# Four small memsets of a constant move from GpSimd to VectorE at the start of a fused attention and gated FFN kernel

## The chip, the cores and the metric

The kernel runs on one core of one Trainium2 chip. The metric is the device time of one launch in microseconds (us). The time before is the median of three runs, 517.77 us (517.19 to 517.79).

The engines are named as in the profile: PE is TensorE's matrix multiplication and PEld its weight load, DVE is VectorE, ACT is ScalarE, POOL is GpSimd, SP is SyncE. [...]

## The reference

Attention with keys and values projected to 64 positions (Linformer), followed by a gated FFN:

```python
# q, k, v: (8, 8, 1024, 64); E, F: (64, 1024); all float32
k_proj = einsum('ks,bhsd->bhkd', E, k)
v_proj = einsum('ks,bhsd->bhkd', F, v)
scores = (1 / sqrt(64)) * matmul(q, k_proj.transpose(0, 1, 3, 2))
attn = softmax(scores)
x = matmul(attn, v_proj).transpose(0, 2, 1, 3).reshape(8192, 512)
gate = 1 / (1 + exp(-(x @ w_gate)))          # w_gate, w_val: (512, 1536)
out = (gate * (x @ w_val)) @ w_out           # w_out: (1536, 512)
```

The output is (8192, 512) in float32.

## The kernel before, in words

**Tiling.** A batch has 1024 positions, which are handled as two blocks of 512 tokens. Per batch the kernel projects k and v with E and F, forms the scores, takes the exponential on ACT, multiplies by the projected v, normalizes, and runs the FFN over the two blocks: 12 column tiles of 128 for the gate and the value, then the output projection. From the second block on, a growing part of the FFN's products is computed in a Strassen-like form with fewer multiplications, with the sums on DVE and copies on ACT. Matmuls are in bf16, with sums in PSUM in float32. The bulk of the kernel (from the third block on) is ordered by a planner with costs and due times (`arranged`). The start, which the change touches, is not: it runs in the order in which the code records it.

**How order and waits come about.** Each operation is recorded by `Plan.add` with keys that it reads (`r`) and writes (`w`). Every engine executes its own operations in the order of recording. `add` looks up, for each key, the writers and readers recorded so far, and makes the new operation wait for them: a read waits for the earlier writer, a write waits for earlier writers and earlier readers. Waits within DVE are left out for a write after a read, waits across engines never are. A DMA counts on a semaphore of its own; other operations that somebody waits for count on their engine's semaphore.

**The start.** The calls come in this order:

```python
start_loads()
blocks_ready(0)
constants()
project_consts()
busy(4)
```

- `start_loads` (L472) issues the loads of E and F on SP (L476). On POOL it sets `quad` by four memsets of 32 partitions each, to 0, 32, 64 and 96 (L482), and then issues 22 loads through `load` (L403): k, q, k, q, v, v for the halves of the heads of batch 0, then pieces of the gate and value weights with two more of q among them.
- `blocks_ready(0)` (L914) sets `kpd`, which is used from batch 2 on, to zero on POOL. It names `quad` among the keys that it reads, though it doesn't touch that tile.
- `constants` (L504) works on DVE alone: `count` (0 to 127 in each row, by doubling, L505 and L509), four patterns (L515 to L533), their transpose `rows` (L545), `row_f` (the partition's number, a row number plus `quad`, L553), the identity matrices `identf` and `ident` (L559), `half` (L567), the selectors `dsel8` (L576), `bsel8f` and `bsel8` (L592).
- `project_consts` (L604) transposes E and F on PE with `identf`; ACT copies the result to `EFT`.
- `busy(n)` (L628) puts n matmuls of `ident` with itself into PE's order; nothing uses their result. Four follow the transposes, and ten more stand between the steps of the first half unit.
- The first half unit then projects k of batch 0 for half of the heads, transposes q and the projected k, forms scores and so on, up to `xT` (L868), the FFN's input. The FFN's first products (L385 with wG and wV) follow.

All matmuls are recorded at L385, all ACT operations of the helper at L389.

Of the kernel before, what the change touches and what calls it, by code (L numbers as in the profile page):

```python
# [121 lines left out]
class Plan:  # L122
# [31 lines left out]
    def add(self, eng, fn, r=(), w=(), x=(), dma=None, t=None, tie=(), pad=0.0):  # L154
        if self.tasks is not None:
            self.note(eng, (eng, fn, tuple(r), tuple(w), tuple(x), dma), t, tie, pad)
            return None
        op = Op()
        op.eng, op.fn, op.dma, op.need = eng, fn, dma, False
        op.sem, op.val = None, 0  # L160
        deps = {}

        def dep(o, raw):
            if o is op:
                return
            if o.eng == eng and o.dma is None:
                if eng == "PE" or (eng != "POOL" and not raw):
                    return
            deps[id(o)] = o

        for k in r:
            for o in self.writers.get(k, ()):
                dep(o, True)
        for k in tuple(w) + tuple(x):
            for o in self.writers.get(k, ()):
                dep(o, False)
            for o in self.readers.get(k, ()):
                dep(o, False)
        for k in r:
            self.readers.setdefault(k, []).append(op)  # L180
        for k in tuple(w) + tuple(x):
            self.writers[k] = [op]
            self.readers[k] = []
        op.deps = list(deps.values())
        for o in op.deps:
            o.need = True
        if dma is not None:
            self.dma_count[dma] = self.dma_count.get(dma, 0) + 16
            op.sem, op.val = dma, self.dma_count[dma]
        self.ops.append(op)  # L190
        return op
# [46 lines left out]
def bass_linformer_attn__then__ffn_glu_sigmoid_kernel(  # L238
# [18 lines left out]
    with contextlib.ExitStack() as es:  # L257

        def sbuf(name, shape, dtype):
            return es.enter_context(nc.sbuf_tensor(name, shape, dtype))  # L260
# [38 lines left out]
        quad = sbuf("quad", [P, 1], FP32)  # L299
# [91 lines left out]
        def dve(fn, r, w, b=None, t=None):  # L391
            x = [] if b is None else [("bank", b)]
            return add("DVE", fn, r=r, w=w, x=x, t=t)

        def pool(fn, r=(), w=()):
            return add("POOL", fn, r=r, w=w)
# [33 lines left out]
        def load_kv_heads(n, src, R):  # L430
            hh = slice(4 * R, 4 * R + 4)
            load(
                KV[n][:, hh, :],
                src[0].rearrange("h (p t) d -> p h (t d)", t=NT)[:, hh, :],
                [("KV", n, R)],
                f"KV{n}{R}",
            )
# [34 lines left out]
        def start_loads():  # L472
            for src, rows, n in ((E, slice(0, 64), "E"), (F, slice(64, 128), "F")):
                add(
                    "SP",
                    lambda e, src=src, rows=rows: e.dma_start(EF[rows, :], src[:, :]),  # L476
                    w=[("EF", n)],
                    dma="in" + n,
                )
            for i in range(4):  # L480
                pool(
                    lambda e, i=i: e.memset(quad[32 * i : 32 * i + 32, :], 32.0 * i),  # L482
                    w=[("quad", i)],
                )
            for R in range(2):
                load_kv_heads(0, k, R)
                load_q_half(0, 0, R)
            for R in range(2):
                load_kv_heads(1, v, R)
            load_w(0, 0)  # L490
            load_w(0, 1)
            load_w(1)
            load_w(2)
            for R in range(2):
                load_q_half(0, 1, R)
            load_w(3)
            load_w(4)
            load_w(5)

        def heads8():  # L500
            x = count[:, 0:8].rearrange("p (h b) -> p h b", h=2)
            return x.unsqueeze(2).to_broadcast([P, 2, 4, 4])

        def constants():  # L504
            dve(lambda e: e.memset(count[:, 0:1], 0.0), [], ["count"])  # L505
            for i in range(7):
                n = 1 << i
                dve(
                    lambda e, n=n: e.tensor_scalar(  # L509
                        count[:, n : 2 * n], count[:, 0:n], float(n), None, op0=ALU.add  # L510
                    ),
                    ["count"],
                    ["count"],
                )
            dve(lambda e: e.tensor_copy(pats[:, 0, :], count[:, 0:32]), ["count"], ["pats"])  # L515
            dve(
                lambda e: e.tensor_copy(
                    pats[:, 1, :].rearrange("p (h a b) -> p h a b", h=2, b=4),
                    heads8(),
                ),  # L520
                ["count"],
                ["pats"],
            )
            dve(
                lambda e: e.tensor_copy(
                    pats[:, 2, :].rearrange("p (a b) -> p a b", b=4),
                    count[:, 0:4].unsqueeze(1).to_broadcast([P, 8, 4]),
                ),
                ["count"],
                ["pats"],  # L530
            )
            dve(
                lambda e: e.tensor_scalar(  # L533
                    pats[:, 3, :].rearrange("p (a b) -> p a b", b=16),
                    count[:, 0:16].unsqueeze(1).to_broadcast([P, 2, 16]),
                    8.0,
                    -1.0,
                    op0=ALU.is_ge,
                    op1=ALU.mult,
                ),  # L540
                ["count"],
                ["pats"],
            )
            dve(
                lambda e: e.transpose(  # L545
                    rows[:, :, :].rearrange("p a b -> p (a b)"),
                    pats[:, :, :].rearrange("p a b -> p (a b)"),
                ),
                ["pats"],
                ["rows"],  # L550
            )
            dve(
                lambda e: e.tensor_tensor(row_f[:, :], rows[:, 0, 0:1], quad[:, :], ALU.add),  # L553
                ["rows"] + [("quad", i) for i in range(4)],
                ["row_f"],
            )
            for t, n in ((identf, "identf"), (ident, "ident")):
                dve(
                    lambda e, t=t: e.tensor_scalar(  # L559
                        t[:, :], count[:, :], row_f[:, 0:1], None, op0=ALU.is_equal  # L560
                    ),
                    ["count", "row_f"],
                    [n],
                )
            for n, op in ((0, ALU.is_ge), (1, ALU.is_lt)):
                dve(
                    lambda e, n=n, op=op: e.tensor_scalar(  # L567
                        half[:, n : n + 1], row_f[:, :], 64.0, None, op0=op
                    ),
                    ["row_f"],  # L570
                    [("half", n)],
                )
            for n in range(2):
                for i in range(4):
                    dve(
                        lambda e, n=n, i=i: e.tensor_scalar(  # L576
                            dsel8[:, n, i, :].rearrange("p (h a b) -> p h a b", h=2, b=4),
                            heads8(),
                            half[:, n : n + 1],
                            2.0 * i,  # L580
                            op0=ALU.subtract,
                            op1=ALU.is_equal,
                        ),
                        ["count", ("half", n)],
                        [("dsel8", n)],
                    )
            for t, k, m, i, v in (
                (bsel8f, "bsel8f", 8, 1, 0.25),
                (bsel8, "bsel8", 8, 1, 0.5),
            ):  # L590
                dve(
                    lambda e, t=t, m=m, i=i, v=v: e.tensor_scalar(  # L592
                        t[:, :, :, :].rearrange("p c h d -> p (c h) d"),
                        count[:, 0:m].unsqueeze(2).to_broadcast([P, m, 64]),
                        rows[:, i, 0:1],
                        v,
                        op0=ALU.is_equal,
                        op1=ALU.mult,
                    ),
                    ["count", "rows"],  # L600
                    [k],
                )
# [1525 lines left out]
```

The softmax here doesn't subtract the row's maximum and nothing guards it: scores larger than these inputs give would overflow.

## Time and profile before

| what | us |
|---|---|
| median of three runs | 517.77 |
| the profiled execution | 517.65 |
| its span | 515.90 |
| PE busy | 505.0 |
| DVE busy | 410.9 |
| ACT busy | 345.0 |
| POOL busy | 41.0 |
| PE's first matmul starts | 5.86 |
| DVE's first instruction starts | 0.82 |
| POOL's quad memsets | 0.75 to 1.31 |
| POOL's memset of kpd | 18.32 to 19.28 |
| v's first half lands | 17.26 |

The span runs from the first to the last thing that the profile shows; the execution's own time is 1.75 us longer. Starts are counted from the span's start. A line of the timeline gives the start, the busy time, the engine, the source line, the operation, the tile written and the one read, the number of instructions, and in brackets how long the engine stood idle and what released it. PE's records overlap, because matmuls are pipelined. A queue name with q at its end (POOLq, SPq) stands for an engine's sequencer. The granted clock of PE is given as 1.0 in all stages.

### The profile page before, as it was taken

The numbers are of one execution on the slowest core, as the hardware profiler recorded it, in microseconds if no ns is written. First come the engines' busy times: TensorE is split into PE (matmuls) and PEld (weight loads), VectorE is DVE, ScalarE is ACT, GpSimd is POOL, SyncE is SP. The second block draws the span as 40 slices with busy tenths as digits, with TensorE's granted clock in tenths as the row PEclk, the third lists the DMA queues.
The fourth block names the chain that finished last, engine by engine and source line by source line (L and its number), as shares of the span: only waits on it lengthen the run. The fifth ranks groups of instructions, "written<-read, shape, count | busy, mean of one in ns | idle before, by whom it ended". The sixth has DMA issues, their size and how long they took to land.

```text
span 515.9 us, 11369 instructions
## 1 busy us (share of the span) xinstructions
PE 505.0 (98%) x4598; PEld 410.0 (79%) x4598; DVE 410.9 (80%) x809; ACT 345.0 (67%) x645; POOL 41.0 (8%) x60
## 2 busy tenths in 40 slices
PE   5999999999999999999999999999999999999996
PEld 3545645888888888888888888888888888888885
DVE  4548779899789796988879888797969898777774
ACT  2555683867778677677767776777676766676652
POOL 9420301200200020000100020000000000000000
PEclk9999999999999999999999999999999999999999
DMA  9999999899798788454946389374104330201013
GB/s 161 199 198 204 150 195 221 115 178 233 93 224 155 152 150 138 102 125 123 174 85 154 60 152 203 56 164 100 46 7 97 42 104 1 83 1 76 6 43 124
DMA packets 105205, 63.13 MB, mean 122 GB/s; under 512 B 63040, under 2 KB 97344, under 8 KB 105152
## 3 DMA queue, kind: packets, MB, share of 16 engines
q0 software_dynamic: 34000, 29.89, 37.5%
q1 hardware_dynamic: 71152, 32.52, 28.8%
q8 instruction: 36, 0.59, 0.4%
q14 instruction: 17, 0.14, 0.1%
HBM read 60.29 MB, written 16.78 MB: 149 GB/s over the span
## 4 chain that ended last, share of the span: by engine, by line
PE 94%; DMA 2%; DVE 1%; POOL 1%; issue 0%; ACT 0%; DVEq 0%; POOLq 0%
PE pA L385 51%; PE pF L385 43%; DMA KVs<-in_v_dram 2%; DVE hT L1832 0%; POOL KVs L403 0%; DVE vsnap L1710 0%; POOL Qb L403 0%; DVE xT L868 0%; DVE ost L1437 0%; ACT sig L389 0%; DVE sig L1786 0%; ACT vsnap L389 0%; DVE ost L1522 0%; POOL quad L482 0%; DVE hS L1382 0%
## 5 line engine op out<-in xcount | busy, mean ns | idle before, releaser
L389 ACT ACTIVATE sig<-pA 128x512 f32<-128x512 f32 x126 | 75.1, 596 | 43.4 <-PE pA L385 42.8
L1699 ACT ACTIVATE pF<-pA 128x512 f32<-128x512 f32 x99 | 58.5, 591 | 30.9 <-PE pA L385 26.3
L1710 DVE TENSOR_TENSOR vsnap<-pF,vsnap 128x512 f32<-128x512 f32 x90 | 61.8, 686 | 18.1 <-ACT vsnap L389 9.2
L1786 DVE TENSOR_TENSOR sig<-pF,sig 128x512 f32<-128x512 f32 x84 | 57.5, 685 | 7.2 <-PE pA L385 3.7
L385 PE MATMUL pF<-wO,hT 128*128 128x256 bf16 (+1 forms) x402 | 59.3, 285 | 0.0
L389 ACT ACTIVATE vsnap<-pA 128x512 f32<-128x512 f32 x84 | 50.2, 597 | 11.9 <-PE pA L385 11.8
L1832 DVE SCALAR_TENSOR_TENSOR hT<-sig,vsnap 128x512 bf16<-128x512 f32 x84 | 56.6, 683 | 0.9
L389 ACT ACTIVATE sig<-sig 128x512 f32<-128x512 f32 x84 | 52.8, 629 | 2.9 <-DVE sig L1786 2.6
L385 PE MATMUL pF<-xS,wV 128*128 128x256 bf16 x360 | 54.0, 273 | 0.1
L385 PE MATMUL pA<-xT,gT 128*128 128x256 bf16 x336 | 50.4, 273 | 0.0
L385 PE MATMUL pF<-xS,wG 128*128 128x256 bf16 x336 | 50.4, 273 | 0.0
L385 PE MATMUL pA<-xT,vT 128*128 128x256 bf16 x336 | 50.4, 273 | 0.0
L385 PE MATMUL pF<-xT,wG 128*128 128x256 bf16 (+1 forms) x264 | 50.2, 311 | 0.2 <-DVE xT L868 0.2
L389 ACT ACTIVATE sig<-pF 128x512 f32<-128x512 f32 x66 | 39.5, 598 | 15.0 <-PE pF L385 13.1
L385 PE MATMUL pA<-wT,hT 128*128 128x256 bf16 x360 | 48.8, 273 | 0.1
L1832 DVE SCALAR_TENSOR_TENSOR hT<-sig,pF 128x512 bf16<-128x512 f32 x42 | 28.7, 683 | 24.6 <-PE pF L385 24.4
L385 PEld LDWEIGHTS pF<-wO,hT 128*128 128x128 bf16 x402 | 38.7, 98 | 10.5 <-issue 0.8
L385 PE MATMUL pF<-xT,wV 128*128 128x256 bf16 (+1 forms) x240 | 41.5, 294 | 0.0
L385 PEld LDWEIGHTS pF<-xS,wV 128*128 128x128 bf16 x360 | 34.9, 98 | 6.1 <-DVE vsnap L1710 0.4
L385 PEld LDWEIGHTS pA<-wT,hT 128*128 128x128 bf16 x360 | 34.3, 98 | 5.6 <-ACT EF L389 0.8
L389 ACT ACTIVATE eT<-pA 128x512 bf16<-128x512 f32 x58 | 34.1, 596 | 5.7 <-PE pA L385 4.4
L385 PEld LDWEIGHTS pA<-xT,vT 128*128 128x128 bf16 x336 | 32.3, 98 | 5.2 <-issue 0.4
(159 smaller groups left out, 906.5 us busy)
## 6 DMA issues: line engine op xcount, KB each, us to landing
out_dram<-ost SPq DMA_DIRECT2D x61, 256.0 KB, 2.5
Qb<-in_q_dram POOLq DMA_DIRECT2D x7, 1024.0 KB, 11.9
KVs<-in_k_dram POOLq DMA_DIRECT2D x7, 1024.0 KB, 13.7
KVs<-in_v_dram POOLq DMA_DIRECT2D x7, 1024.0 KB, 18.0
wO<-in_moe_w_out_dram POOLq DMA_DIRECT2D x2, 768.0 KB, 9.8
wG<-in_moe_w_gate_dram POOLq DMA_DIRECT2D x5, 256.0 KB, 18.9
wV<-in_moe_w_val_dram POOLq DMA_DIRECT2D x5, 256.0 KB, 19.4
KVs<-in_k_dram POOLq DMA_DIRECT2D x2, 512.0 KB, 9.3
```

The costliest lines, as they stand in the source:

```text
L385: return add("PE", lambda e: e.matmul(o, lhsT, rhs, **kw), r=r, x=[("bank", b)])
L389: return add("ACT", lambda e: e.activation(o, i, func, scale=scale), r=r, w=w, x=x, t=t)
L1699: lambda e: e.activation(bank[c][:, :], bank[a][:, :], AF.Copy, scale=1.0),
L1710: lambda e: e.tensor_tensor(o, bank[bk][:, :], o, ALU.add),
L1786: dve(lambda e: e.tensor_tensor(o, bank[bk][:, :], o, ALU.add), [key], [key], b=bk)
L1832: lambda e: e.scalar_tensor_tensor(o, sg.rearrange("p (j c) -> p j c", j=2), 1.0, x.rearrange("p (j c) -> p j c", j=2), ALU.add, ALU.mult,),
```

## The change

The four memsets of `quad` are taken out of `start_loads`, where POOL ran them ahead of its first load, and are put at the head of `constants`, on DVE. The calls and their order stay as they are, and so do the keys.

```diff
@@ start_loads
-            for i in range(4):
-                pool(
-                    lambda e, i=i: e.memset(quad[32 * i : 32 * i + 32, :], 32.0 * i),
-                    w=[("quad", i)],
-                )
             for R in range(2):
                 load_kv_heads(0, k, R)
                 load_q_half(0, 0, R)
@@ constants
         def constants():
+            for i in range(4):
+                dve(
+                    lambda e, i=i: e.memset(quad[32 * i : 32 * i + 32, :], 32.0 * i),
+                    [],
+                    [("quad", i)],
+                )
             dve(lambda e: e.memset(count[:, 0:1], 0.0), [], ["count"])
```

The memset of `kpd` is not touched by it:

```python
pool(lambda e: e.memset(kpd[:, :, :, :], 0.0), [("quad", i) for i in range(4)], [("kpd", 0), ("kpd", 1), "preset"])
```

## The prediction

> **What bounds the kernel now.** I read the page first, then the start of the span engine by engine in order of time, then the chain of waits.
>
> The page's busy shares come first (engine, busy us, share of the span, instructions).
>
> ```profile
> PE 505.0 (98%) x4598; PEld 410.0 (79%) x4598; DVE 410.9 (80%) x809; ACT 345.0 (67%) x645; POOL 41.0 (8%) x60
> ```
>
> TensorE (PE) is busy 505.0 of 515.9 us, so 10.9 us are idle. The table of stages splits the beginning:
>
> ```profile
> 0.00:5.86 5.86, 0.01 (x1) 0.04 (x1) 4.66 (x28) 1.28 (x1) 5.11 (x14) 1.00 0.63 128
> 5.86:23.87 18.01, 17.09 (x198) 9.85 (x199) 7.52 (x19) 8.26 (x18) 13.38 (x18) 1.00 1.32 195
> 23.87:48.00 24.13, 24.13 (x178) 11.47 (x179) 14.49 (x27) 12.64 (x23) 2.64 (x3) 1.00 1.36 202
> ```
>
> After the stretch and its length comes PE's busy time, then those of PEld, DVE, ACT and POOL. More than half of all PE idleness is the 5.86 us before its first matmul; from 23.87 us on PE has no gap to absorb anything. So whatever delays PE's first matmul delays the end by about as much, unless the 18 us after it hold waits that then vanish. Their idle part is 18.01 - 17.09 = 0.92 us.
>
> What PE waits for up to 30 us (total us, times, longest):
>
> ```profile
> PE pA L385 <- DMA EF<-in_F_dram: 5.9, 1, 5.9
> PE pA L385 <- DMA KVs<-in_k_dram: 0.5, 1, 0.5
> ```
>
> The first is the landing of F; E, F and VectorE's identity matrix (identf, L559) are what the first transposes need. On VectorE (DVE) the identity is made at the very start (start us, busy us):
>
> ```profile
> 0.82 0.06 DVE L505 MEMSET vT<- 128x1 f32 x1 [0.82 <-PEq L2113]
> ...
> 3.45 0.16 DVE L553 TENSOR_TENSOR row_f<-gT,quad 128x1 f32<-128x1 f32 x1
> 3.64 0.29 DVE L559 TENSOR_SCALAR vT<-vT,row_f 128x128 f32<-128x128 f32 x1
> ```
>
> identf is done at 3.64 + 0.29 = 3.93 us, 1.93 us before F lets PE go. That slack is all the chain has. On GpSimd (POOL):
>
> ```profile
> 0.75 0.56 POOL L482 MEMSET quad<- 32x1 f32 x4 [0.29 <-POOLq L2113]
> 1.36 0.89 POOL L403 DMA_DIRECT2D KVs<-in_k_dram  x1
> ...
> 17.40 0.88 POOL L403 DMA_DIRECT2D wV<-in_moe_w_val_dram  x1
> 18.32 0.96 POOL L914 MEMSET kpd<- 128x1024 bf16 x1
> ```
>
> The quad memsets hold the first keys from 0.75 to 1.36 us. Twenty-two issues stand ahead of the memset of kpd at 18.32 us, for which the plan notes that it reads quad (L914).
>
> **What the Trainium skill says.** "Trainium Architecture — The Big Picture", Inside one NeuronCore: each engine runs its own instruction stream, and streams meet only at semaphores. The trace agrees: DVE begins at 0.82 us beside POOL's 0.75 us. "SBUF — State Buffer", Who interferes with whom: VectorE's copies and tensor-scalar operations in a two-port mode and GpSimd's descriptor writing exclude each other, and the loser waits for the whole instruction. The trace fits: the POOL issue that starts at 5.16 us takes 1.41 us where its neighbours take 0.72 to 0.79 us, and DVE runs its two 128x512 operations of L592 from 5.40 to 6.27 us. "TensorE: Matmul & The Clock Gate", What's actually happening: the array starts at half rate and is released by a free-running activity window of about 3.4 us. The trace shows the slow phase: matmuls of the K projection start 0.107 us apart per pair up to 10.1 us, and weight loads take 178 ns there against 106 ns later, so it lasted about 4.2 us after PE's start.
>
> **The change, part by part.**
>
> (1) POOL loses four memsets. The first issue moves from 1.36 to 0.75 us, 0.61 us earlier, and all initial loads with it.
>
> (2) DVE gains four 32x1 memsets. The trace has no such row on DVE; the nearest is the 128x1 memset, 0.06 us. Bounds: 4 x 0.06 = 0.24 and, at the 0.09 us distance to the next instruction (0.82 to 0.91), 0.36 us. I take 0.24. Beside DVE's slack of 1.93 us that would cost nothing. It is not the decisive part.
>
> (3) A wait appears. The order in which the plan records operations is loads, then blocks_ready(0) with the kpd memset, then constants(). Before, the kpd memset followed the writers of quad; it read what they had written. Now it is recorded ahead of them, and still names quad as something it reads. So the first quad memset on DVE becomes a write after a read: it must wait for POOL's kpd memset. The compiled order of the changed kernel shows exactly this: DVE's first instruction, the quad memset, waits on POOL's semaphore, the kpd memset has lost its wait, L553 waits on DVE alone, and every other row of all engines is the same. The semaphore's first increment is the kpd memset, since no earlier POOL instruction but DMAs remains and those count on their own semaphores. Queued behind the waiting instruction is all of DVE: count, pats, rows, row_f, identf, ident, half, dsel8, bsel8. Behind identf stand PE's transposes of E and F, and behind those the whole kernel. The 1.93 us of slack is exceeded many times over.
>
> When does the kpd memset end? Before, 18.32 + 0.96 = 19.28 us. From that go 0.61 us of part (1). DVE is now silent while POOL issues, so the long second v issue should fall back from a distance of 1.40 us (5.16 to 6.56) to 0.73 us as its neighbours have: 0.67 us. That is 18.00 us. Bounds: 18.67 if the long issue has another cause; 17.85 if the first issue's distance of 0.88 us also becomes 0.73.
>
> From there to PE: hand-over 0.06 us (DVE's kpD copy ends at 12.15, its matmul starts at 12.21); four memsets 0.24; count to identf took 3.93 - 0.82 = 3.11 us; hand-over 0.06. In those 3.11 us four 128x32 operations (2.49 to 2.75 us) all finish just after 3.00, when the issue of 2.24 us ends (2.24 + 0.76), and one of L509 takes 0.30 us where its kind takes 0.17 to 0.20. Without POOL beside it that is at most 0.27 us less; I take 2.95, bounds 2.84 and 3.11. Sum: 18.00 + 0.06 + 0.24 + 2.95 + 0.06 = 21.31 us, against 5.86: PE starts 15.45 us late. Bounds of this: 15.2 and 16.4.
>
> (4) What is given back. All first loads have landed by then or land ahead of use: k's second half landed at 13.4, v's first at 17.26, both before 21.31. The 0.52 us wait for k at 12.95 us goes, and so does 0.10 us for v (fillers end at 17.21, v's matmuls start at 17.31): 0.62 us; bounds 0.52 and 0.75, the 0.92 us less the 0.16 us for xT, which is DVE's. The filler matmuls (L630) stand in the order and run whether there is a wait or not, so they give nothing back. The rest of the constants ended 2.34 us after identf (6.27 - 3.93), and DVE is next needed 5.5 us after PE's start (11.37): hidden. SP's loads of E and F stay at 0.75 and 1.38 us and now land long before their use. Later loads (q, k, v of batch 1, wO) stand behind the kpd memset on POOL and on SP, but wait for PE or its results, so they move with PE.
>
> (5) The clock's slow phase comes again, 15 us later. By the page named, it may last 3.4 to 6.8 us instead of 4.2, and half of a slow microsecond is lost at most: -0.4 to +1.3 us, an estimate; I take 0.
>
> Sum: +15.45 - 0.62 = +14.83 us. Nothing later is free to absorb it. Span 515.90 + 14.83 = 530.73 us. The profiled execution had 517.65 us, 1.75 around its span; the median of the runs is 517.77, 0.12 above. So 517.77 + 14.83 = 532.6 us. Bounds: 15.2 - 0.75 - 0.4 = 14.05, 531.8 us; 16.4 - 0.52 + 1.3 = 17.2, 535.0 us.
>
> **The rivals.**
>
> A, faster: the edit does what it says. If the first quad memset on DVE didn't have to wait for kpd (the point that decides: whether that semaphore is reached only after POOL's last issue), DVE would finish identf at about 4.2 us, under the 5.86 us of F, and the keys would come up to 0.61 us sooner. PE would lose at most its 0.62 us of waits: 517.77 - 0.6 = 517.2 us, within what a measurement can tell from no change (0.2%, 1.0 us). For it: the initial POOL issues lie in the chain that ended last, up to the landing of v. Against: the compiled wait. 0.03.
>
> B, a smaller loss: the stage after PE's start hides more waiting for data than PE's gaps show. Weight loads (PEld) stood idle for k 1.8 us, for q 0.4 and for v 0.6, 2.8 us in all. If all of that were time for data and not for the fillers queued ahead, 2.8 us would return: 15.45 - 2.8 = +12.65, 530.4 us. Against: PE's own records fill those times but for 0.62 us. 0.09.
>
> C, a larger loss: the long issue doesn't shorten (+0.67), DVE's chain stays at 3.11 (+0.16), and the slow phase is long (+1.3): +17.0 us, 534.7 us or more. 0.10.
>
> **How the numbers follow.** Main case 0.78; A 0.03, B 0.09, C 0.10. The predicted time is the main case's. The range 531.8 to 534.8 us takes the bounds of the unknown costs nearly to their ends and holds the main case and part of C, somewhat over 8 in 10. Faster by over 0.2%: in A the gain is about 0.1%, so 0.01; within 0.2%: 0.02; slower: 0.97.
>
> **What would show it.** In the changed kernel's trace: POOL's first key issue near 0.75 us; the kpd memset from about 17.0 to 18.0 us; no DVE instruction before that, four quad memsets right after; identf near 21.2 us; PE's first matmul near 21.3 us, released by DVE and not by F; no wait for k or v before PE's first wG matmuls; the stretch from PE's first matmul to the first gap-free wG stream (5.86 to 23.87 before) about 17.4 us long; from there the same 492 us to the end. A DVE that starts at 0.8 us would prove the reading of the wait wrong; a stretch near 15.2 us would be B.

## The result, and the profile after

The changed kernel takes 533.09 us (median of five runs, 532.75 to 533.78) against 517.77 us (median of five, 517.19 to 518.90): slower, by a ratio of 1.0296 (95% interval 1.0282 to 1.0310). The forecast was 532.6 us in a range of 531.8 to 534.8. The profiled execution took 532.75 us, its span 531.0, which is 15.1 us more than the span of before. Lines that both kernels share carry a number one higher in the changed kernel from L505 on.

First the stages of the changed kernel, cut at PE's first matmul and at the start of the gap-free wG stream; the third is cut after the same length as before (columns as before: stretch, length, then busy time and count of PE, PEld, DVE, ACT and POOL):

```profile
0.00:22.03 22.03, 0.00 (x0) 0.03 (x1) 2.85 (x21) 1.28 (x1) 17.48 (x27) 1.00 1.11 176
22.03:38.96 16.93, 16.66 (x198) 9.77 (x199) 9.31 (x30) 8.26 (x18) 0.00 (x0) 1.00 1.29 175
38.96:63.09 24.13, 24.13 (x178) 11.47 (x179) 14.49 (x27) 12.64 (x23) 2.64 (x3) 1.00 0.69 104
```

The first stage grew from 5.86 to 22.03 us, the second shrank from 18.01 to 16.93 us, and the third shows the same counts and busy times of all engines as those 24.13 us before. What follows 38.96 us lasts 531.0 - 38.96 = 492.0 us, as the 515.9 - 23.87 = 492.0 us of before. So the whole change is +16.17 - 1.08 = +15.09 us, and it lies in the first two stages.

What PE waits for up to 30 us in the changed kernel:

```profile
PE pA L385 <- DVE vT L560: 22.0, 1, 22.0
```

F is no longer what lets PE go; identf (L560) is. VectorE at its start, and the identity:

```profile
18.58 0.40 DVE L502 MEMSET quad<- 32x1 f32 x4 [18.58 <-POOL kpd L915]
19.04 0.06 DVE L506 MEMSET vT<- 128x1 f32 x1
...
21.41 0.16 DVE L554 TENSOR_TENSOR row_f<-gT,quad 128x1 f32<-128x1 f32 x1
21.60 0.29 DVE L560 TENSOR_SCALAR vT<-vT,row_f 128x128 f32<-128x128 f32 x1
```

The bracket in the first line is the case in one line: VectorE stands idle for 18.58 us, released by POOL's memset of kpd. And POOL:

```profile
1.25 0.89 POOL L403 DMA_DIRECT2D KVs<-in_k_dram  x1 [0.80 <-POOLq L2114]
...
16.66 0.90 POOL L403 DMA_DIRECT2D wV<-in_moe_w_val_dram  x1
17.39 1.13 POOL L915 MEMSET kpd<- 128x1024 bf16 x1
```

The memset of kpd ends at 17.39 + 1.13 = 18.52 us and VectorE starts 0.06 us later. (Its record overlaps that of the issue ahead, which ends at 16.66 + 0.90 = 17.56 us; from there it takes 0.96 us, as before.) The first key issue moved from 1.36 to 1.25 us, and not to 0.75 us.

### The profile page after: what moved, and what is told of

Same layout as the page of the kernel before. It is cut to its first block, busy times and chain, and to the rows that moved or that the text cites. A ratio compares the mean times of both kernels' runs of the same rounds, so it can differ in the third digit from the quotient of the medians.

```text
span 531.0 us, 11368 instructions
## 1 busy us (share of the span) xinstructions
PE 504.5 (95%) x4598; PEld 409.9 (77%) x4598; DVE 410.8 (77%) x813; ACT 345.2 (65%) x645; POOL 40.0 (8%) x56
## 4 chain that ended last, share of the span: by engine, by line
PE 94%; POOL 3%; DVE 2%; issue 0%; ACT 0%; DVEq 0%; POOLq 0%
PE pA L385 50%; PE pF L385 43%; POOL wV L403 1%; POOL wG L403 1%; POOL KVs L403 1%; POOL Qb L403 1%; DVE hT L1833 0%; DVE vsnap L1711 0%; DVE vT L510 0%; POOL kpd L915 0%; DVE xT L869 0%; DVE ost L1438 0%; ACT sig L389 0%; DVE sig L1787 0%; ACT vsnap L389 0%
```

## The experiments

The theory: the write-after-read wait of VectorE's first instruction on kpd's memset is the whole loss, and its price is set by where that memset stands in POOL's order and by what is queued behind the wait on VectorE. The rival: the moved memsets themselves are the cost, on VectorE or by what they do to GpSimd. All ratios are to the kernel before, with 95% intervals, and the diffs are shortened. A read-after-write wait is that of a reader for the writer ahead of it; a write-after-read wait is that of a writer for a reader recorded ahead of it.

**e1_no_key: the wait taken away, the memsets still on VectorE.** kpd doesn't touch quad, so the key can go.

```diff
-pool(memset(kpd), [("quad", i) for i in range(4)], [("kpd", 0), ("kpd", 1), "preset"])
+pool(memset(kpd), [], [("kpd", 0), ("kpd", 1), "preset"])
```

> The changed kernel, but the memset of kpd no longer names quad as something it reads, so no wait stands ahead of VectorE's first instruction; the memsets stay on VectorE. Theory (the write-after-read wait on kpd is the whole cause): VectorE starts near 0.8 us, identf ends near 4.4 us under F's landing, PE starts near 5.9 us, and the first key issue stays near 1.25 us as in the changed kernel, 0.11 us earlier than before: 517.2 to 517.9 us, no measurable difference from before. Rival (four memsets on VectorE, or GpSimd without them, are themselves the cost): about 533 us.

Measured: 516.9 us, ratio 0.9985 (0.9977 to 0.9993), just under the expected span of times. VectorE in this kernel:

```profile
0.81 0.40 DVE L502 MEMSET quad<- 32x1 f32 x4 [0.81 <-PEq L2114]
...
4.28 0.29 DVE L560 TENSOR_SCALAR vT<-vT,row_f 128x128 f32<-128x128 f32 x1
```

The memsets run on VectorE at 0.81 us and identf is there at 4.57 us, ahead of F. The rival falls: the move itself costs nothing. With the wait gone the kernel measures 0.15% under the one before. Of the kernels below that are also free of the wait, e5_two_two measures 0.13% and e7_swap 0.04%, so a gain of this size stays open.

**e2_wait_alone: the wait added to the kernel before, the memsets left on GpSimd.**

```diff
-pool(memset(kpd), [("quad", i) for i in range(4)], ...)
+pool(memset(kpd), [("quad", i) for i in range(4)] + ["held"], ...)
...
-dve(lambda e: e.memset(count[:, 0:1], 0.0), [], ["count"])
+dve(lambda e: e.memset(count[:, 0:1], 0.0), [], ["count", "held"])
```

> The kernel before, with the four memsets of quad left on GpSimd; only a key is added, so that VectorE's first instruction (the memset of count) must wait for the memset of kpd, as the changed kernel's does. Theory: kpd ends near 18.8 us (first issue at 1.36, the long second v issue back to 0.73 us because VectorE is silent), PE starts near 21.8 us, 1.1 us are given back in the stretch after it: 532.4 to 533.0 us. Rival (the moved memsets are the cost): about 517.8 us.

Measured: 532.59 us, ratio 1.0289 (1.0275 to 1.0303). In its trace the memset of count starts at 18.73 us, released by kpd, and PE at 21.73 us, released by identf. The wait alone gives the loss, 15.1 of the changed kernel's 15.3 us. PE starts 0.3 us earlier than in the changed kernel: the memsets of quad (0.46 us there) are not behind the wait, and kpd's memset ends at 18.66 instead of 18.52 us.

**e3_kpd_mid: the same wait, kpd's memset after six issues instead of 22.**

```diff
@@ start_loads
             for R in range(2):
                 load_kv_heads(1, v, R)
+            blocks_ready(0)
             load_w(0, 0)
@@ the calls
-        blocks_ready(0)
         constants()
```

> The changed kernel with the same wait, but the memset of kpd stands after the first six issues (k, q, k, q, v, v) instead of after all 22. Theory (the place of kpd in GpSimd's order sets the price): kpd ends near 6.9 us, PE starts near 10.6 us, 4.7 us later than before; 0.6 to 1.1 us are given back: 521.3 to 522.0 us. Rival (a fixed price of the edit, independent of the queue ahead): about 533 us.

Measured: 522.2 us, ratio 1.0087 (1.0073 to 1.0101), 0.2 us above the expected times. The price follows the place in the queue. What was missed is on VectorE:

```profile
6.88 0.40 DVE L503 MEMSET quad<- 32x1 f32 x4 [6.88 <-POOL kpd L916]
7.34 0.06 DVE L507 MEMSET vT<- 128x1 f32 x1
7.44 2.14 DVE L511 TENSOR_SCALAR vT<-vT 128x1 f32<-128x1 f32 x7
...
10.91 0.28 DVE L561 TENSOR_SCALAR vT<-vT,row_f 128x128 f32<-128x128 f32 x1
```

The wait ends when expected (6.88 us), but from count to identf VectorE takes 11.19 - 7.34 = 3.85 us, where it took 2.85 us in the changed kernel. Here POOL is issuing the weights beside it; the part on the port below has the lines that tie the two together.

**e4_kpd_first: the same wait, kpd's memset ahead of all loads.**

```diff
-        start_loads()
         blocks_ready(0)
+        start_loads()
         constants()
```

> The changed kernel with the same wait, but the memset of kpd is GpSimd's first instruction, ahead of all loads. Theory: the wait ends near 1.8 us, identf near 5.4 us, still under F's landing at 5.86 us; what remains is that the loads start near 1.85 instead of 1.36 us, which PE meets at its waits for k: +0.2 to +0.8 us, 518.0 to 518.6 us. Rival (fixed price): about 533 us.

Measured: 518.24 us, ratio 1.0015 (1.0006 to 1.0023). The wait is still there and ends at 1.75 us; PE starts at 5.84 us, released by F. The same wait costs about 15 us, 4.7 us or under 1 us by its place alone. The loads start at 1.64 us, not at 1.85. That is still 0.28 us later than before, and PE's second key projection starts 0.23 us later (13.70 against 13.47).

**e7_swap: constants recorded ahead of kpd's memset, the key kept.**

```diff
-        blocks_ready(0)
         constants()
+        blocks_ready(0)
```

> The changed kernel with the memsets on VectorE and kpd still naming quad, but the two calls exchanged, so that kpd is recorded after the writers of quad, and waits for VectorE instead of the reverse. Theory (only the direction of the wait costs): the same as without the key, 516.6 to 517.4 us, kpd's wait long satisfied when GpSimd gets there near 17.9 us. Rival (any tie between kpd and quad across engines costs): 520 us or more.

Measured: 517.08 us, ratio 0.9996 (0.9989 to 1.0003). Now kpd waits for VectorE, whose memsets of quad end at 1.21 us, long before GpSimd reaches kpd at 17.94. A tie between the two engines is harmless in this direction. The gain of e1_no_key can't be told here from no change; the two kernels differ by 0.2 us, less than their runs spread. The profiled loads scatter by more than that too: the second half of k is issued at 2.87 us in e1 and 2.88 in e7, and lands 10.3 and 9.5 us later.

**e8_late_quad: the wait kept, the four memsets just ahead of their only reader.** They move within `constants` from the head to just before L553 (row_f).

> The changed kernel with its wait, but the four memsets stand on VectorE just ahead of row_f, their only reader, instead of at its head: count, patterns and rows are then made before the wait. Theory (the waiting instruction costs what is queued behind it on VectorE): identf follows kpd's end by 0.06 + 0.46 + 0.5 us instead of 3.4, PE starts 2.3 us earlier than in the changed kernel, 530.5 to 531.1 us. Rival (VectorE's own chain is hidden, only kpd's end counts): 533 us.

Measured: 531.02 us, ratio 1.0256 (1.0240 to 1.0272), about 2.1 us under the changed kernel. VectorE:

```profile
3.71 0.31 DVE L540 STREAM_TRANSPOSE gT<-vT 128x128 f32<-128x128 f32 x1
18.57 0.40 DVE L549 MEMSET quad<- 32x1 f32 x4 [14.56 <-POOL kpd L915]
19.01 0.16 DVE L554 TENSOR_TENSOR row_f<-gT,quad 128x1 f32<-128x1 f32 x1
19.20 0.29 DVE L560 TENSOR_SCALAR vT<-vT,row_f 128x128 f32<-128x128 f32 x1
```

The same wait ends at the same time, but count, patterns and rows lie ahead of it. PE starts at 19.64 instead of 22.03 us. An engine's order is part of the price of a wait: 2.4 us of the changed kernel's late start were work that needed no quad.

**e5_two_two and e6_eight: why the first issue came at 1.25 us.** One has two memsets on GpSimd and two on VectorE (kpd names only the first two), the other does the four memsets twice on GpSimd.

> Two of the four memsets (quad 0 and 1) on GpSimd ahead of its loads, two on VectorE; kpd names only the two of GpSimd, so VectorE has no wait. It asks why the first key issue came at 1.25 us without any memset on GpSimd, where 0.75 us was forecast. Theory (the first issue needs until about 1.25 us whatever stands ahead, and memsets up to then run beside that): first issue again at 1.25 us though the memsets end near 1.0 us. Rival (the issue follows the last memset at once, and a queue without memsets is a case of its own): first issue near 1.1 us. Either way 516.7 to 517.8 us.

> The kernel before with the four memsets of quad done twice on GpSimd, eight in all, ahead of its loads. Theory (beyond about 1.25 us memsets delay the first issue one for one): first issue near 1.9 us, 0.55 us later than before, met by PE at its waits for k and v: 517.9 to 518.4 us. Rival (the start of the loads is hidden): 517.5 us.

Measured: 516.66 us, ratio 0.9987 (0.9978 to 0.9996), and 518.11 us, ratio 1.0009 (1.0000 to 1.0018). POOL's first lines, first with two memsets, then with eight:

```profile
0.75 0.23 POOL L482 MEMSET quad<- 32x1 f32 x2 [0.29 <-POOLq L2119]
1.31 0.89 POOL L403 DMA_DIRECT2D KVs<-in_k_dram  x1 [0.33 <-issue]
```

```profile
0.75 1.19 POOL L482 MEMSET quad<- 32x1 f32 x8 [0.29 <-POOLq L2113]
1.83 0.89 POOL L403 DMA_DIRECT2D KVs<-in_k_dram  x1
```

With none, two, four and eight memsets the first issue starts at 1.25, 1.31, 1.36 and 1.83 us. Up to four, each adds 0.03 us; with two, POOL stands idle for 0.33 us between memsets and issue. So the first issue is not ready before some 0.5 us after POOL is free, and the memsets of before ran almost wholly inside that time (0.75 to 1.31 us). The theory of e5 holds but for those 0.06 us; what POOL's sequencer does in that half microsecond, the traces don't show. In e6 the four further memsets delay the first issue by 0.47 us, a little less than the 0.55 expected. PE meets the later keys as expected, with 1.0 us of waits for k instead of 0.5, and its second key projection starts at 14.02 instead of 13.47 us. The interval of e6's time just reaches 1.0000, so its cost shows in the trace more clearly than in the time.

## Why the prediction was right, step by step

**The mechanism (part 3) held.** e1_no_key takes the wait away and the loss is gone; e2_wait_alone adds only the wait and the loss is there; e3 and e4 move its end and the loss follows.

**Its terms.** All are from the two profiled executions. The numbers in brackets after a term are the parts of the prediction.

| term | forecast us | measured us |
|---|---|---|
| first issue earlier (1) | 0.61 | 0.11 |
| long second v issue shortens | 0.67 | 0.67 (5.07 to 5.80) |
| kpd's memset after the last issue | 0.96 | 0.96 (17.56 to 18.52) |
| end of kpd's memset | 18.00 | 18.52 |
| hand-over to VectorE | 0.06 | 0.06 |
| four memsets on VectorE (2) | 0.24 | 0.46 (18.58 to 19.04) |
| count to identf | 2.95 | 2.85 (19.04 to 21.89) |
| hand-over to PE | 0.06 | 0.14 |
| PE's first matmul | 21.31 | 22.03 |
| given back after it (4, 5) | 0.62 | 1.08 |
| sum | +14.83 | +15.09 |

The two sums differ by 0.26 us (the medians by 0.5), but that hides two larger misses of opposite sign: PE started 0.72 us later than forecast, and 0.46 us more came back. That they offset each other was luck.

**The mis-sized terms.** The miss in part (1) is the largest, 0.50 us: "The first issue moves from 1.36 to 0.75 us" counted the memsets' time as delay of the issue, but most of it lay beside the half microsecond that the first issue needs anyway (e5, e6). Part (2) used the 0.06 us of one memset as its distance to the next; four 32x1 memsets start 0.11 to 0.12 us apart, and the stated upper bound of 0.36 us was too low. The hand-over to PE, for which the prediction took the 0.06 us of another pair of operations, was 0.14 us. PE's whole delay, 16.17 us, still lies within the stated 15.2 to 16.4.

**The port.** The forecast that the long v issue shortens once VectorE is silent was right, and e1_no_key shows the other side. There VectorE runs its two operations of L593 from 6.04 to 6.91 us, and POOL's issue that begins at 5.79 us is now the long one:

```profile
4.33 1.53 POOL L403 DMA_DIRECT2D KVs<-in_v_dram  x2
5.79 1.28 POOL L403 DMA_DIRECT2D wG<-in_moe_w_gate_dram  x1
7.05 0.72 POOL L403 DMA_DIRECT2D wV<-in_moe_w_val_dram  x1
```

In every kernel that runs these two operations while POOL is issuing, one issue beside them takes 1.22 to 1.43 us: the second of v before and in e6, the first of wG in e1, e5 and e7, the first of wV in e4, one of q in e3. In the changed kernel, e2 and e8 they run after the last issue, and no issue takes more than 0.92 us. So the long issue follows VectorE's operation and not a place in POOL's queue, as the section of "SBUF — State Buffer" named in the prediction has it.

VectorE loses too. Its chain from count to identf takes 2.85 us alone (changed kernel), 3.11 us beside the first issues (before) and 3.85 us in e3. Where its 128x32 operations (L515 to L533 before) are held up, they end with the issue under way, as here in e1, at 3.64 us:

```profile
3.16 0.48 DVE L516 COPY vT<-vT 128x32 f32<-128x32 f32 x1
```

```profile
2.87 0.77 POOL L403 DMA_DIRECT2D KVs<-in_k_dram  x1
```

Before, both end at 3.00 us, and in e3 at 10.31 us. Two engines can thus hold each other up without a semaphore between them.

**What was given back (4, 5).** The second stage lasts 18.01 us before, 17.20 us in e2, 17.19 in e3, 17.31 in e8 and 16.93 us in the changed kernel. In e2, as in the changed kernel, the data are there when PE asks for them. By PE's lines the 0.81 us between before and e2 are 0.11 at the first k (PE's start to the K projection 3.58 against 3.69), 0.05 in that projection, 0.66 up to the second k, with q ahead of it (2.38 against 3.04), and 0.16 at v (3.68 against 3.84), less 0.17 at the step after it. There the gain at v is lost again: PE's products with eT take 0.62 instead of 0.46 us, and the exponential on ACT that they read ends at 32.94 us, 0.17 after their start, where before the two coincide (17.89 and 17.88).

So waits give back 0.76 us where part (4) said 0.62. It had counted PE's idle records alone, 0.52 for k and 0.10 for v, and left out the first k and q. The rest of the 1.08 us goes with the length of the K projection, which part (5) had put at 0. By kernel (before, e2, changed kernel):

```profile
9.55 0.95 PE L385 MATMUL pA<-KVs,EFT 128*64 128x128 bf16 x16
```

```profile
25.31 0.90 PE L385 MATMUL pA<-KVs,EFT 128*64 128x128 bf16 x16
```

```profile
25.61 0.64 PE L385 MATMUL pA<-KVs,EFT 128*64 128x128 bf16 x16
```

The same 16 matmuls take 0.64 us later in each run and up to 1.06 us (e4 to e7) in the slow phase. By the spacing of the matmuls, the phase was over at the latest 3.6 us after PE's start in the changed kernel (25.61 - 22.03), after some 4.3 us before, 5.4 us in e5 and e7, and 6.0 us in e6. (The clock column of the stage tables, 1.00 throughout, doesn't show it.) These lengths fit the free-running window that the prediction cited and its -0.4 to +1.3 us, but no run here set the phase on purpose, so that cause stays argued and not shown, and that the phase was short in the changed kernel, which gave back some 0.3 us, is luck as far as these runs tell.

**The rivals.** A's time, 517.2 us, is what e1_no_key and e7_swap give (516.9 and 517.08) once the wait is gone; in the changed kernel the wait was there. B asked for 2.8 us back and 1.08 came, so most of PEld's idle time was not time for data. C needed the long issue to stay and the slow phase to be long, and neither happened.

## What to carry to other kernels

When an operation moves to another engine, read who names its tile as input or output between the old place and the new one in the recorded order: moving the writer past a reader turns a harmless read-after-write into a write-after-read, and across engines that is a real wait. Price the wait by two queues: what stands ahead of the releasing instruction on its engine (here 22 issues) and what stands behind the waiting one (here all the constants and, through them, PE). The repair costs nothing: drop a key that is no real use of the tile, or record the writer first.

## What the runs showed that was not expected

- The first DMA issue of GpSimd starts about 0.5 us after the engine is free for it (1.25 against 0.75 us), and up to four small memsets ahead of it cost 0.03 us each, where they start 0.14 us apart.
- Small memsets of 32 partitions on VectorE start 0.11 to 0.12 us apart, at 0.06 us of busy time each.
- GpSimd's issues and VectorE's operations hold each other up, and which one pays differs. One POOL issue beside VectorE's two 128x512 operations took 1.22 to 1.43 us where most take 0.7 to 0.9, while VectorE's 128x32 operations, where they were held up, ended with POOL's issue. VectorE's chain of constants took 2.85 us alone and 2.85 (e6) to 3.85 us (e3) beside POOL's issues.
